# Block 0 of a convolution-and-feed-forward kernel: loads in order of need, weight rounding in three steps, and another product split over the column groups

## Chip, cores, metric

One core of a Trainium2 chip. The metric is the device time of one execution in microseconds, as the median of several. All timed runs are of the state "fast" (granted clock 0.999 to 1.0); single executions are so marked.

## The reference

```
# x (8, 4096, 192), weight (8, 7), w_in (192, 2048), w_out (2048, 192)
w = softmax(weight)                         # over the 7 taps of each of 8 heads
y[b, t, d] = sum_k w[head(d), k] * x[b, t - 6 + k, d]      # causal convolution
h = y @ w_in                                # 32768 tokens
out = (h * clip(h + 3, 0, 6) / 6) @ w_out
```

The weights of the feed-forward part come as float64 and are rounded to float32 on the chip.

## The kernel before

The tokens are worked on in 32 blocks of 1024. In each block VectorE makes the convolution `y`, TensorE makes 16 chunks of `h` (two row groups at a time), ScalarE and VectorE the activation ("Relu", then "gate"), and TensorE the out phase (four column groups of 32 at a time; from block 1 on by seven Strassen products of half-size matrices in place of eight plain ones). Block 0 differs: the weights are still arriving and are rounded in 16 units of 128 x 384 elements: 8 of `w_in`, 8 of `w_out`.

```python
class Rounding:                                  # before: two steps
    def first(self):
        ...
        nc.vector.tensor_scalar(out=self.scale[:], in0=high, ...)     # split: two
        nc.vector.tensor_scalar(out=self.top[:], in0=high, ...)       # instructions
        nc.scalar.activation(over[:], self.scale[:], ACT.Relu, ...)   # three passes
        nc.scalar.activation(self.scale[:], over[:], ACT.Relu, ...)
        nc.scalar.mul(self.rest[:], low, 2.0**-52)
    def second(self):
        nc.vector.scalar_tensor_tensor(out=self.scale[:], ...)        # join: two
        nc.vector.scalar_tensor_tensor(out=self.sig[:], ...)          # instructions
        nc.gpsimd.tensor_tensor(out=self.dst, in0=self.sig[:], in1=self.scale[:].bitcast(F32), op=ALU.mult)
        self.then()                              # w_in units: swap

def swap():      # the halves of a w_in unit change places: two DMAs within SBUF
    nc.sync.dma_start(out=w_in[D2:P, other], in_=w_in[0:D2, own])
    nc.sync.dma_start(out=w_in[0:D2, other], in_=w_in[D2:P, own])

def advance(n):                                  # split and passes of a later unit,
    for _ in range(n):                           # then the join of this one
        begin()
        next(ended).second()
...
    for s in range(K3):                          # first round: four chunks, four banks
        for c, h in early:
            h_mm(0, c, h, s)
    for n, (c, h) in enumerate(early):
        h_out(c, h)                              # Relu and gate
        if n:
            advance(1)
    for p in range(2, NP):                       # the other twelve chunks
        h_unit(0, p)
        advance(1)
        h_unit(0, NP + p)
        if p < 5:
            advance(1)
```

Of the kernel before, what the change touches and what calls it, by code (L numbers as in the profile page):

```python
# [7 lines left out]
ALU = mybir.AluOpType  # L8
# [7 lines left out]
def kernel(  # L16
# [49 lines left out]
    ps = ctx.enter_context(tc.tile_pool(name="ps", bufs=4, space=bass.MemoryType.PSUM))  # L66
    start_pools = ExitStack()
    stg = start_pools.enter_context(tc.tile_pool(name="stg", bufs=2 * NP))
    cnv = start_pools.enter_context(tc.tile_pool(name="cnv", bufs=3))

    def load_x(i):
        b, t0 = i // BPB, (i % BPB) * TB
        x = xs.tile([P, K3, PAD + N], F32, name="x")
        src = xT[b].rearrange("(p s) t -> p s t", s=K3)
        head = PAD if t0 == 0 else 0
        if head:
            nc.vector.memset(x[0:D2, :, 0:PAD], 0.0)
        nc.sync.dma_start(out=x[0:D2, :, head:], in_=src[..., t0 - PAD + head : t0 + N])
        nc.sync.dma_start(out=x[D2:P, :, :], in_=src[..., t0 + N - PAD : t0 + TB])
        return x  # L80


# [4 lines left out]
            in_=weight.unsqueeze(1).to_broadcast([H, GJ, KC]),  # L87
        )

    x_tiles = {0: load_x(0)}  # L90



# [15 lines left out]
    def load_w_in(dma, j):  # L109
        st = stage()  # L110
        for half in range(2):
            dma.dma_start(  # L112
                out=st[half * D2 : (half + 1) * D2].rearrange("p (s f) w -> p s (f w)", s=K3),
                in_=w_in_bits[j + half * NP].rearrange("p s f w -> p s (f w)"),
            )
        return st

    def load_w_out(dma, j):
        st = stage()
        dma.dma_start(  # L120
            out=st[:].rearrange("p (k d) w -> p k (d w)", k=2), in_=w_out_bits[:, j]
        )
        return st
# [6 lines left out]
    class Rounding:  # L130
# [7 lines left out]
        def __init__(self, st, dst, then):  # L138
            self.st, self.dst, self.then = st, dst, then

        def first(self):
            low, high = self.st[:, :, 0], self.st[:, :, 1]
            self.rest = cnv.tile([P, WS], F32, name="rest")
            self.top = cnv.tile([P, WS], U32, name="top")
            self.sig = cnv.tile([P, WS], F32, name="sig")
            self.scale = cnv.tile([P, WS], U32, name="scale")
            over = cnv.tile([P, WS], F32, name="over")
            nc.vector.tensor_scalar(  # L148
                out=self.scale[:], in0=high, scalar1=0x7FF00000, scalar2=None,
                op0=ALU.bitwise_and,  # L150
            )
            nc.vector.tensor_scalar(
                out=self.top[:], in0=high, scalar1=0xFFFFF, scalar2=0x100000,
                op0=ALU.bitwise_and, op1=ALU.bitwise_or,
            )


            nc.scalar.activation(  # L158
                over[:], self.scale[:], ACT.Relu, bias=bias_e[:, 0:1], scale=-1.0
            )  # L160
            nc.scalar.activation(  # L161
                self.scale[:], over[:], ACT.Relu, bias=bias_e[:, 1:2], scale=-8.0
            )
            nc.scalar.mul(self.rest[:], low, 2.0**-52)  # L164

        def second(self):
            nc.vector.scalar_tensor_tensor(
                out=self.scale[:], in0=self.st[:, :, 1], scalar=0x80000000,
                in1=self.scale[:], op0=ALU.bitwise_and, op1=ALU.bitwise_or,
            )  # L170
            nc.vector.scalar_tensor_tensor(
                out=self.sig[:], in0=self.top[:], scalar=2.0**-20, in1=self.rest[:],
                op0=ALU.mult, op1=ALU.add,
            )
            nc.gpsimd.tensor_tensor(
                out=self.dst, in0=self.sig[:], in1=self.scale[:].bitcast(F32), op=ALU.mult
            )
            self.then()
# [17 lines left out]
                out=w_out[:, :, o], in0=w_out[:, :, x], in1=w_out[:, :, y], op=ALU.subtract  # L196
            )

    w_in_st = [load_w_in(nc.scalar if j < 2 else nc.sync, j) for j in range(NP)]
    w_out_st = [load_w_out(nc.sync, j) for j in range(NP)]  # L200

    mx = cst.tile([P, 1], F32, name="mx")
    nc.vector.tensor_reduce(out=mx[:], in_=w_sb[:], axis=AX.X, op=ALU.max)
# [3 lines left out]
    )  # L207
    nc.scalar.activation(e_sb[:], e_sb[:], ACT.Exp)
    sm = cst.tile([P, 1], F32, name="sm")
    nc.vector.tensor_reduce(out=sm[:], in_=e_sb[:], axis=AX.X, op=ALU.add)  # L210
    nc.vector.tensor_scalar_add(sm[:], sm[:], 1e-9)
    nc.vector.reciprocal(sm[:], sm[:])
    c_sb = cst.tile([P, KC], F32, name="c_sb")
    half = cst.tile([P, 1], F32, name="half")
    nc.vector.memset(half[:], 0.5)
# [40 lines left out]
                start=(s == 0), stop=(s == K3 - 1),  # L256
            )

    def h_out(c, h):

        r6 = rs.tile([P, G, N], F32, name="r6")
        nc.scalar.activation(r6[:], h[:], ACT.Relu, bias=half[:], scale=1.0 / 6.0)  # L262
        nc.vector.scalar_tensor_tensor(  # L263
            out=g[:, c % NP, c // NP], in0=r6[:], scalar=1.0, in1=h[:],
            op0=ALU.min, op1=ALU.mult,
        )

    def h_unit(i, c):
        h = banks()
        for s in range(K3):  # L270
            h_mm(i, c, h, s)
        h_out(c, h)

    def dff_half(k):
        return g[:, :, k // G, k % G]
# [13 lines left out]
    def side_by_side(*streams):  # L289
        for mms in zip(*streams):  # L290
            for m in mms:
                m()
# [36 lines left out]
    def out_strassen(i, conv):  # L329

        prod = {
            1: (A11, B11), 2: (A12, B21), 3: (S4, B22), 4: (A22, T4),
            5: (S1, T1), 6: (S2, T2), 7: (S3, T3),
        }

        def product(bank, j, n, q, ks=every):
            return mm(bank, j, *prod[n], q, ks, True, True)

        def three(n, n4, q4):
            bank = banks()[:, 0]  # L340
            side_by_side(
                *[product(bank, q, n, q) for q in range(NQ)], product(bank, NQ, n4, q4)
            )
            return bank

        def piece(dst, q, src, j):
            nc.scalar.copy(  # L347
                out=dst[q * QS : (q + 1) * QS], in_=src[j * QS : (j + 1) * QS]
            )

        def add(out, x, y, op=ALU.add):
            nc.vector.tensor_tensor(out=out, in0=x, in1=y, op=op)  # L352

        def store(c, k, half_):

            xt = ot.tile([P, N], F32, name="xt")
            nc.vector.transpose(out=xt[0:DH], in_=c)  # L357
            for q in range(NQ):
                store_rows(i, k, half_ * NQ + q, xt, q)

        m = slice(0, DH)
        p1, p2, p4, p5, u2, u3 = (cs.tile([DH, N], F32, name=f"c{k}") for k in range(6))
        b = three(1, 2, 0)
        nc.scalar.copy(out=p1[:], in_=b[m])  # L364
        piece(p2, 0, b, NQ)
        s_sums(every, (2, 4), 4)
        b = three(4, 2, 1)
        nc.scalar.copy(out=p4[:], in_=b[m])  # L368
        piece(p2, 1, b, NQ)
        for u in conv[:4]:  # L370
            u()
        n = NP // 4
        b = banks()[:, 0]
        side_by_side(*[product(b, j, 2, 2, range(j * n, (j + 1) * n)) for j in range(4)])
        last = p2[2 * QS : 3 * QS]
        piece(p2, 2, b, 0)
        for j in range(1, 4):
            add(last, last, b[j * QS : (j + 1) * QS])
        add(p2[:], p1[:], p2[:])
        store(p2[:], 0, 0)  # L380
        for u in conv[4:]:
            u()
        b7 = three(7, 5, 0)
        piece(p5, 0, b7, NQ)
        b = three(6, 5, 1)
        piece(p5, 1, b, NQ)
        add(u2[:], p1[:], b[m])
        add(u3[:], u2[:], b7[m])
        add(p4[:], u3[:], p4[:], ALU.subtract)
        store(p4[:], 1, 0)  # L390
        b = three(3, 5, 2)
        piece(p5, 2, b, NQ)
        add(u2[:], u2[:], b[m])
        add(u2[:], u2[:], p5[:])
        store(u2[:], 0, 1)
        add(u3[:], u3[:], p5[:])
        store(u3[:], 1, 1)

    def s_sums(pairs, which, width):

# [11 lines left out]
    for j in range(4):  # L412
        units += [w_out_unit(j, w_out_st[j]), w_in_unit(4 + j, w_in_st[4 + j])]
    units += [w_out_unit(j, w_out_st[j]) for j in range(4, NP)]
    begun = iter(units)
    ended = iter(units)

    def begin():
        u = next(begun, None)
        if u:  # L420
            u.first()

    def advance(n):
        for _ in range(n):
            begin()
            next(ended).second()

    with tc.manual_schedule():
        begin()
        begin()  # L430
        nc.vector.tensor_tensor(
            out=c_sb[:], in0=e_sb[:], in1=sm[:].to_broadcast([P, KC]), op=ALU.mult
        )
        next(ended).second()
        next(ended).second()
        conv0 = conv_units(0, [slice(s, s + 1) for s in range(K3)])
        for s in range(K3):
            for u in conv0[s * KC : (s + 1) * KC]:
                u()
            advance(1) if s else begin()  # L440
        x_tiles[1] = load_x(1)


        early = [(c, banks()) for p in range(2) for c in (p, NP + p)]
        for s in range(K3):
            for c, h in early:
                h_mm(0, c, h, s)
        for n, (c, h) in enumerate(early):
            h_out(c, h)
            if n:  # L450
                advance(1)
        for p in range(2, NP):
            h_unit(0, p)
            advance(1)
            h_unit(0, NP + p)
            if p < 5:
                advance(1)
        y_tiles.pop(0)
        w_out_sums()
        start_pools.close()  # L460
# [52 lines left out]
```

## Time and profile before

| | before |
|---|---|
| time, median | 2548.4 us |
| TensorE waits for the first swap, then starts its long run | 32.12 us |
| out phase of block 0 starts | 92.20 us |
| block 0 ends | 133.60 us |
| 31 blocks of | 77.59 us |
| last matmul to the end | 8.3 us |

The table is read from the chain of waits (the work that ended last, followed back from the last instruction, at each step to what released it) and from the busy times by stage; the prediction shows the lines. From 133.60 us to the last matmul TensorE never waits, so a change that takes no matmuls away can win only ahead of that and behind it.

### The profile page before, as it was taken

Reading aid. Unit: us, or ns where it says so; the run is one execution under the profiler, and the core shown is the slowest. Engines: PE = TensorE matmul, PEld = TensorE weight load, DVE = VectorE, ACT = ScalarE, POOL = GpSimd, SP = SyncE. Lnnn points to the kernel's source line nnn. Section 1 sums busy time; section 2 is a strip of 40 time slices with the busy share of each in tenths; the row PEclk is TensorE's granted clock in tenths of the full one; section 3 lists DMA queues with packets and bytes.
Section 4 is the critical chain, followed back from the end, with each engine's and each line's share of the span. In section 5 each row is a group of like instructions: output and inputs, shape, how many; then the busy total and the mean of one; then the engine's idle time right before and its main releaser. Section 6 shows DMA issues by size and latency. Waiting matters only on the chain.

```text
span 2547.2 us, 37923 instructions
## 1 busy us (share of the span) xinstructions
PE 2495.4 (98%) x16944; PEld 945.9 (37%) x16944; DVE 1923.2 (76%) x1640; ACT 740.9 (29%) x810; POOL 28.6 (1%) x24
## 2 busy tenths in 40 slices
PE   4899999999999999999999999999999999999998
PEld 2233333333333333333333333333333333333333
DVE  5667777777778777877777787777787787777775
ACT  3333222332222332223332223322233322233222
POOL 1300000000000000000000000000000000000000
PEclk9999999999999999999999999999999999999999
DMA  6001110011110111101111101111001111011100
GB/s 142 16 17 26 26 26 7 19 26 26 26 22 8 23 26 26 26 8 21 24 26 26 26 5 22 26 26 26 12 18 23 26 26 26 7 20 26 26 13 13
DMA packets 223155, 60.91 MB, mean 24 GB/s; under 512 B 204560, under 2 KB 210704, under 8 KB 222992
## 3 DMA queue, kind: packets, MB, share of 16 engines
q1 hardware_dynamic: 222088, 57.70, 12.1%
q8 instruction: 133, 2.18, 0.4%
q10 hardware_dynamic: 904, 0.79, 0.2%
q14 instruction: 30, 0.25, 0.0%
HBM read 31.72 MB, written 25.17 MB: 22 GB/s over the span
## 4 chain that ended last, share of the span: by engine, by line
PE 97%; ACT 1%; DMA 1%; issue 1%; DVE 0%; ACTq 0%; SPq 0%; DVEq 0%
PE banks L254 51%; PE banks L281 46%; ACT r L262 0%; DMA stage<-in_moe_w_in_dram 0%; DMA w_in<-w_in 0%; DMA stage<-in_moe_w_out_dram 0%; ACT over L158 0%; ACT rest L164 0%; ACT scale L161 0%; DVE g L263 0%; DVE scale L148 0%; SPq L112 0%; DVE c L352 0%; ACTq L112 0%; ACTq L85 0%
## 5 line engine op out<-in xcount | busy, mean ns | idle before, releaser
L254 PE MATMUL banks<-y,w_in 64*128 64x512 f32 x6144 | 1334.4, 591 | 43.4 <-DVE y L231 23.7
L263 DVE SCALAR_TENSOR_TENSOR g<-r,banks 128x1024 f32<-128x1024 f32 x512 | 623.3, 1218 | 428.6 <-ACT r L262 428.6
L254 PEld LDWEIGHTS banks<-y,w_in 64*128 64x128 f32 x6144 | 598.1, 187 | 779.2 <-issue 751.7
L262 ACT ACTIVATE r<-banks,half 128x1024 f32<-128x1024 f32 x512 | 569.9, 1114 | 789.5 <-PE banks L254 723.8
L281 PE MATMUL banks<-g,w_out 128*32 128x512 f32 x6336 | 739.4, 593 | 0.0
L281 PE MATMUL banks<-s,w_out 128*32 128x512 f32 x4464 | 643.6, 592 | 0.0
L281 PEld LDWEIGHTS banks<-g,w_out 128*32 128x32 f32 x6336 | 215.4, 110 | 516.1 <-issue 491.5
L231 DVE SCALAR_TENSOR_TENSOR y<-x,c_sb,y 128x1536 f32<-128x1536 f32 (+1 forms) x204 | 356.1, 1745 | 6.1
L281 PEld LDWEIGHTS banks<-s,w_out 128*32 128x32 f32 x4464 | 183.5, 110 | 296.8 <-issue 296.5
L347 ACT COPY c<-banks 32x512 f32<-32x512 f32 x186 | 107.7, 579 | 601.6 <-PE banks L281 600.9
L352 DVE TENSOR_TENSOR c<-c,banks 32x512 f32<-32x512 f32 (+1 forms) x186 | 127.4, 685 | 138.9 <-ACT c L347 133.8
L409 DVE TENSOR_TENSOR g<-g 128x1024 f32<-128x1024 f32 x124 | 151.9, 1225 | 4.3
L409 DVE TENSOR_TENSOR s<-g 128x1024 f32<-128x1024 f32 x124 | 151.9, 1225 | 4.2
L409 DVE TENSOR_TENSOR s<-g,s 128x2048 f32<-128x2048 f32 x62 | 139.1, 2284 | 0.0
L409 DVE TENSOR_TENSOR s<-s,g 128x2048 f32<-128x2048 f32 x62 | 139.0, 2284 | 0.0
L357 DVE STREAM_TRANSPOSE xt<-c 96x512 f32<-96x512 f32 x124 | 87.7, 707 | 4.3
L352 DVE TENSOR_TENSOR c<-c,c 96x512 f32<-96x512 f32 x124 | 83.9, 677 | 3.2
L364 ACT COPY c<-banks 96x512 f32<-96x512 f32 x31 | 18.0, 582 | 184.0 <-PE banks L281 184.0
L368 ACT COPY c<-banks 96x512 f32<-96x512 f32 x31 | 18.0, 582 | 176.4 <-PE banks L281 176.4
L227 DVE TENSOR_SCALAR y<-x,c_sb 128x1536 f32<-128x1536 f32 (+1 forms) x34 | 57.4, 1689 | 0.0
L158 ACT ACTIVATE over<-scale,bias_e 128x384 f32<-128x384 uint32 x16 | 9.9, 617 | 41.0 <-DVE scale L148 41.0
L325 DVE STREAM_TRANSPOSE xt<-banks 128x512 f32<-128x512 f32 x3 | 2.1, 715 | 17.1 <-PE banks L281 17.1
(25 smaller groups left out, 80.3 us busy)
## 6 DMA issues: line engine op xcount, KB each, us to landing
out_dram<-xt SPq DMA_DIRECT2D x384, 64.0 KB, 2.0
x<-in_x_dram SPq DMA_DIRECT2D x56, 388.5 KB, 5.6
x<-in_x_dram SPq DMA_DIRECT2D x8, 384.0 KB, 4.5
stage<-in_moe_w_out_dram SPq DMA_DIRECT2D x8, 384.0 KB, 7.6
stage<-in_moe_w_in_dram SPq DMA_DIRECT2D x12, 192.0 KB, 6.1
w_in<-w_in SPq DMA_DIRECT2D x16, 96.0 KB, 2.2
stage<-in_moe_w_in_dram ACTq DMA_DIRECT2D x4, 192.0 KB, 8.7
w_sb<-in_weight_dram ACTq DMA_DIRECT2D x1, 1.8 KB
```

The costliest lines, as they stand in the source:

```text
L227: nc.vector.tensor_scalar(out=y[:, part], in0=x[:, part, 0:N], scalar1=c, scalar2=None, op0=ALU.mult)
L231: nc.vector.scalar_tensor_tensor(out=y[:, part], in0=x[:, part, k : k + N], scalar=c, in1=y[:, part], op0=ALU.mult, op1=ALU.add,)
L254: nc.tensor.matmul(out=h[:, k], lhsT=w_in[r, slot, s, :], rhs=y[r, s, :], start=(s == 0), stop=(s == K3 - 1),)
L262: nc.scalar.activation(r6[:], h[:], ACT.Relu, bias=half[:], scale=1.0 / 6.0)
L263: nc.vector.scalar_tensor_tensor(out=g[:, c % NP, c // NP], in0=r6[:], scalar=1.0, in1=h[:], op0=ALU.min, op1=ALU.mult,)
L281: lambda p=p: nc.tensor.matmul(out=bank[j * QS : (j + 1) * QS], lhsT=w_out[:, p, w, cols], rhs=x[:, p], start=(first and p == ps_[0]), sto ...
L347: nc.scalar.copy(out=dst[q * QS : (q + 1) * QS], in_=src[j * QS : (j + 1) * QS])
L352: nc.vector.tensor_tensor(out=out, in0=x, in1=y, op=op)
L357: nc.vector.transpose(out=xt[0:DH], in_=c)
L364: nc.scalar.copy(out=p1[:], in_=b[m])
L368: nc.scalar.copy(out=p4[:], in_=b[m])
L409: nc.vector.tensor_tensor(out=o[:, r], in0=x[:, r], in1=y[:, r], op=op)
```

## The change

Three parts. The loads: weight units in the order in which they are rounded, x of block 0 in three pieces of each half, the first beside unit 0. The rounding: three steps (split, clamp, join) that work on three different units in one turn. The out phase: another product has its last third spread over the four column groups, so that less work follows the last matmul. Its core:

```diff
-    x_tiles = {0: load_x(0)}
+    load_x0(nc.scalar, 0)                       # one third of x of block 0
...
-    w_in_st = [load_w_in(nc.scalar if j < 2 else nc.sync, j) for j in range(NP)]
-    w_out_st = [load_w_out(nc.sync, j) for j in range(NP)]
+    for j in range(NP):
+        w_in_st[j] = load_w_in(nc.sync, j)
+        if j == 1:
+            for s in range(1, K3):
+                load_x0(nc.sync, s)
+        if j >= 4:
+            w_out_st[j - 4] = load_w_out(nc.sync, j - 4)
+    for j in range(4, NP):
+        w_out_st[j] = load_w_out(nc.sync, j)
...
+            r6 = h_relu(h)
+            if slot >= 2 and n < len(units):
+                clamp(n + 1)                    # ScalarE: three passes
+                units[n].join()                 # VectorE: two, then POOL's multiply
+                split(n + 2)                    # VectorE: two
+                n += 1
+            h_gate(c, h, r6)
...
-        side_by_side(*[product(b, j, 2, 2, range(j * n, (j + 1) * n)) for j in range(4)])
+        side_by_side(*[product(b, j, 5, 2, range(j * n, (j + 1) * n)) for j in range(4)])
...
-        b = three(3, 5, 2)
-        piece(p5, 2, b, NQ)
+        b = three(3, 2, 2)
         add(u2[:], u2[:], b[m])
-        add(u2[:], u2[:], p5[:])
-        store(u2[:], 0, 1)
-        add(u3[:], u3[:], p5[:])
-        store(u3[:], 1, 1)
+        store(u2, 0, 1)
+        add(p2[last], p1[last], b[NQ * QS :])
+        store(p2, 0, 0, range(2, NQ))
```

More of the change, by code (lines that the diff above doesn't have):

```diff
@@ L68, with x_source, load_x @@
     stg = start_pools.enter_context(tc.tile_pool(name="stg", bufs=2 * NP))
-    cnv = start_pools.enter_context(tc.tile_pool(name="cnv", bufs=3))
-    def load_x(i):
+    cnv = start_pools.enter_context(tc.tile_pool(name="cnv", bufs=4))
+    def x_source(i):
         b, t0 = i // BPB, (i % BPB) * TB
-        x = xs.tile([P, K3, PAD + N], F32, name="x")
         src = xT[b].rearrange("(p s) t -> p s t", s=K3)
         head = PAD if t0 == 0 else 0
+        return head, src[..., t0 - PAD + head : t0 + N], src[..., t0 + N - PAD : t0 + TB]
+    def load_x(i):
+        x = xs.tile([P, K3, PAD + N], F32, name="x")
+        head, lower, upper = x_source(i)
         if head:
             nc.vector.memset(x[0:D2, :, 0:PAD], 0.0)
-        nc.sync.dma_start(out=x[0:D2, :, head:], in_=src[..., t0 - PAD + head : t0 + N])
-        nc.sync.dma_start(out=x[D2:P, :, :], in_=src[..., t0 + N - PAD : t0 + TB])
+        nc.sync.dma_start(out=x[0:D2, :, head:], in_=lower)
+        nc.sync.dma_start(out=x[D2:P, :, :], in_=upper)
         return x
@@ L88, with load_x0 @@
         )
-    x_tiles = {0: load_x(0)}
+    x_tiles = {0: xs.tile([P, K3, PAD + N], F32, name="x")}
+    nc.vector.memset(x_tiles[0][0:D2, :, 0:PAD], 0.0)
+    def load_x0(dma, s):
+        head, lower, upper = x_source(0)
+        dma.dma_start(out=x_tiles[0][0:D2, s, head:], in_=lower[:, s])
+        dma.dma_start(out=x_tiles[0][D2:P, s, :], in_=upper[:, s])
+    load_x0(nc.scalar, 0)
     w_in = cst.tile([P, NC, K3, P], F32, name="w_in")
@@ L139, in __init__, with split @@
             self.st, self.dst, self.then = st, dst, then
-        def first(self):
-            low, high = self.st[:, :, 0], self.st[:, :, 1]
-            self.rest = cnv.tile([P, WS], F32, name="rest")
+        def split(self):
+            high = self.st[:, :, 1]
             self.top = cnv.tile([P, WS], U32, name="top")
+            self.scale = cnv.tile([P, WS], U32, name="scale")
             self.sig = cnv.tile([P, WS], F32, name="sig")
-            self.scale = cnv.tile([P, WS], U32, name="scale")
-            over = cnv.tile([P, WS], F32, name="over")
             nc.vector.tensor_scalar(
@@ L155, in first, with clamp, join @@
             )
+        def clamp(self):
             nc.scalar.activation(
-                over[:], self.scale[:], ACT.Relu, bias=bias_e[:, 0:1], scale=-1.0
+                self.sig[:], self.scale[:], ACT.Relu, bias=bias_e[:, 0:1], scale=-1.0
             )
             nc.scalar.activation(
-                self.scale[:], over[:], ACT.Relu, bias=bias_e[:, 1:2], scale=-8.0
+                self.scale[:], self.sig[:], ACT.Relu, bias=bias_e[:, 1:2], scale=-8.0
             )
-            nc.scalar.mul(self.rest[:], low, 2.0**-52)
-        def second(self):
+            nc.scalar.mul(self.sig[:], self.st[:, :, 0], 2.0**-52)
+        def join(self):
             nc.vector.scalar_tensor_tensor(
@@ L171, in second @@
             nc.vector.scalar_tensor_tensor(
-                out=self.sig[:], in0=self.top[:], scalar=2.0**-20, in1=self.rest[:],
+                out=self.sig[:], in0=self.top[:], scalar=2.0**-20, in1=self.sig[:],
                 op0=ALU.mult, op1=ALU.add,
@@ L197, in w_out_sums @@
             )
-    w_in_st = [load_w_in(nc.scalar if j < 2 else nc.sync, j) for j in range(NP)]
-    w_out_st = [load_w_out(nc.sync, j) for j in range(NP)]
+    w_in_st, w_out_st = {}, {}
+    for j in range(NP):
[7 more added lines that the diff above has]
+        w_out_st[j] = load_w_out(nc.sync, j)
     mx = cst.tile([P, 1], F32, name="mx")
@@ L209 @@
     sm = cst.tile([P, 1], F32, name="sm")
-    nc.vector.tensor_reduce(out=sm[:], in_=e_sb[:], axis=AX.X, op=ALU.add)
-    nc.vector.tensor_scalar_add(sm[:], sm[:], 1e-9)
-    nc.vector.reciprocal(sm[:], sm[:])
     c_sb = cst.tile([P, KC], F32, name="c_sb")
@@ L257, in h_mm, with h_relu, h_gate @@
             )
-    def h_out(c, h):
+    def h_relu(h):
         r6 = rs.tile([P, G, N], F32, name="r6")
         nc.scalar.activation(r6[:], h[:], ACT.Relu, bias=half[:], scale=1.0 / 6.0)
+        return r6
+    def h_gate(c, h, r6):
         nc.vector.scalar_tensor_tensor(
@@ L271, in h_unit @@
             h_mm(i, c, h, s)
-        h_out(c, h)
+        h_gate(c, h, h_relu(h))
     def dff_half(k):
@@ L352, in add, with store @@
             nc.vector.tensor_tensor(out=out, in0=x, in1=y, op=op)
-        def store(c, k, half_):
+        def store(c, k, half_, qs=range(NQ)):
             xt = ot.tile([P, N], F32, name="xt")
-            nc.vector.transpose(out=xt[0:DH], in_=c)
-            for q in range(NQ):
+            r = slice(qs[0] * QS, (qs[-1] + 1) * QS)
+            nc.vector.transpose(out=xt[r], in_=c[r])
+            for q in qs:
                 store_rows(i, k, half_ * NQ + q, xt, q)
@@ L373, in out_strassen @@
         b = banks()[:, 0]
-        side_by_side(*[product(b, j, 2, 2, range(j * n, (j + 1) * n)) for j in range(4)])
-        last = p2[2 * QS : 3 * QS]
-        piece(p2, 2, b, 0)
+        side_by_side(*[product(b, j, 5, 2, range(j * n, (j + 1) * n)) for j in range(4)])
+        last = slice(2 * QS, 3 * QS)
+        piece(p5, 2, b, 0)
         for j in range(1, 4):
-            add(last, last, b[j * QS : (j + 1) * QS])
-        add(p2[:], p1[:], p2[:])
-        store(p2[:], 0, 0)
+            add(p5[last], p5[last], b[j * QS : (j + 1) * QS])
+        first = slice(0, 2 * QS)
+        add(p2[first], p1[first], p2[first])
+        store(p2, 0, 0, range(2))
         for u in conv[4:]:
@@ L388, in out_strassen @@
         add(u3[:], u2[:], b7[m])
+        add(u2[:], u2[:], p5[:])
         add(p4[:], u3[:], p4[:], ALU.subtract)
-        store(p4[:], 1, 0)
-        b = three(3, 5, 2)
-        piece(p5, 2, b, NQ)
+        store(p4, 1, 0)
+        add(u3[:], u3[:], p5[:])
+        store(u3, 1, 1)
+        b = three(3, 2, 2)
         add(u2[:], u2[:], b[m])
-        add(u2[:], u2[:], p5[:])
-        store(u2[:], 0, 1)
-        add(u3[:], u3[:], p5[:])
-        store(u3[:], 1, 1)
+        store(u2, 0, 1)
+        add(p2[last], p1[last], b[NQ * QS :])
+        store(p2, 0, 0, range(2, NQ))
     def s_sums(pairs, which, width):
@@ L414, with split, clamp @@
     units += [w_out_unit(j, w_out_st[j]) for j in range(4, NP)]
-    begun = iter(units)
-    ended = iter(units)
-    def begin():
-        u = next(begun, None)
-        if u:
-            u.first()
-    def advance(n):
-        for _ in range(n):
-            begin()
-            next(ended).second()
-    with tc.manual_schedule():
-        begin()
-        begin()
+    def split(n):
+        if n < len(units):
+            units[n].split()
+    def clamp(n):
+        if n < len(units):
+            units[n].clamp()
+    with tc.manual_schedule():
+        split(0)
+        clamp(0)
+        nc.vector.tensor_reduce(out=sm[:], in_=e_sb[:], axis=AX.X, op=ALU.add)
+        nc.vector.tensor_scalar_add(sm[:], sm[:], 1e-9)
+        nc.vector.reciprocal(sm[:], sm[:])
         nc.vector.tensor_tensor(
@@ L433 @@
         )
-        next(ended).second()
-        next(ended).second()
         conv0 = conv_units(0, [slice(s, s + 1) for s in range(K3)])
-        for s in range(K3):
-            for u in conv0[s * KC : (s + 1) * KC]:
-                u()
-            advance(1) if s else begin()
+        for k, u in enumerate(conv0):
+            if k == 3:
+                units[0].join()
+                split(1)
+                clamp(1)
+            elif k and k % KC == 0:
+                n = k // KC
+                units[n].join()
+                split(n + 1)
+                clamp(n + 1)
+            u()
+        units[3].join()
+        split(4)
+        clamp(4)
+        split(5)
         x_tiles[1] = load_x(1)
@@ L447 @@
                 h_mm(0, c, h, s)
-        for n, (c, h) in enumerate(early):
-            h_out(c, h)
-            if n:
-                advance(1)
-        for p in range(2, NP):
-            h_unit(0, p)
-            advance(1)
-            h_unit(0, NP + p)
-            if p < 5:
-                advance(1)
+        n = 4
+        for slot in range(2 * NP):
+            c = slot // 2 + slot % 2 * NP
+            if slot < len(early):
+                h = early[slot][1]
+            else:
+                h = banks()
+                for s in range(K3):
+                    h_mm(0, c, h, s)
+            r6 = h_relu(h)
+            if slot >= 2 and n < len(units):
+                clamp(n + 1)
+                units[n].join()
+                split(n + 2)
+                n += 1
+            h_gate(c, h, r6)
+        assert n == len(units)
         y_tiles.pop(0)
```

## The prediction

> **What bounds the kernel now.** I read the chain of waits first. Here are its pieces in order of time (start, length, what):
>
> ```profile
> 32.12 10.39 PE banks L254 x35
> ...
> 92.27 41.34 PE banks L281 x384
> 133.60 41.40 PE banks L254 x192
> 175.01 36.19 PE banks L281 x336
> ...
> 2502.65 36.23 PE banks L281 x336
> 2538.91 0.59 ACT c L347
> ```
>
> From 133.60 to 2538.91 us TensorE never waits: 31 blocks of 41.40 + 36.19 = 77.59 us, 2405.3 us in all. What a change can win without taking matmuls away lies in the other 143 us: block 0, which ends at 133.60 though its matmuls need only 41.4 + 41.3 = 82.7 us, and the 8.3 us after the last matmul (span 2547.2). Next, the busy time by stage (length; then PE, PEld, DVE, ACT and POOL with their counts):
>
> ```profile
> 0.00:32.12 32.12, 2.04 (x3) 0.50 (x3) 18.66 (x40) 8.17 (x14) 3.78 (x7) 1.00 0.99 232
> 32.12:45.06 12.94, 12.94 (x48) 9.99 (x48) 6.94 (x12) 3.79 (x5) 1.00 (x1) 1.00 0.38 92
> 45.06:92.20 47.14, 33.79 (x146) 13.98 (x145) 30.55 (x56) 29.13 (x44) 10.14 (x11) 1.00 0.08 18
> ```
>
> There are three losses. (1) 32.1 us in which TensorE has next to nothing and DMA is busy 0.99 of the time. (2) A first round of four chunks that takes 12.9 us. (3) 47.1 us for the other twelve chunks, which at 41.40 / 16 = 2.59 us each need 31.0; so 16.1 us are lost there. What ends (1) is seen in the timeline and in the answer for the swap's line:
>
> ```profile
> 23.98 0.53 SPq L184 DMA_DIRECT2D w_in<-w_in  x1
> 32.12 21.24 PE L254 MATMUL banks<-y,w_in 64*128 64x512 f32 x82 [6.43 <-DMA w_in<-w_in]
> DMA to landing us min/median/max: 2.1/2.1/8.1
> ```
>
> The first chunk needs the half-swapped copy of weight unit 0. That swap is issued at 23.98, after all 20 weight loads on the same queue, and lands after 8.1 us instead of the usual 2.1, because it stands behind the loads under way. Loss (3) is this loop, once for each chunk, in the chain of waits from 49 to 60 us:
>
> ```profile
> 50.28 0.36 DVE scale L148
> ...
> 50.67 0.63 ACT over L158
> ...
> 51.38 0.62 ACT scale L161
> 52.00 0.45 ACT rest L164
> 52.45 1.01 ACT r L262
> ...
> 53.54 1.07 issue
> 54.62 0.36 DVE scale L148
> ```
>
> 54.62 - 50.28 = 4.34 us a turn. VectorE splits a unit, ScalarE makes three passes over it, only then the chunk's own Relu, then VectorE's gate, then the next split. No engine is full (DVE 30.6, ACT 29.1 of 47.1 us): it is a loop of latency.
>
> **What the Trainium skill says.** "DMA: Bandwidth & Descriptors", section "Queues, rings and completion order", says that each DMA engine consumes its ring in order: the trace agrees (swap 8.1 us behind loads, 2.1 us alone). "SBUF — State Buffer", section "Door 1: The DMA port swizzle", says a transfer over 64 partitions gets the bandwidth of one over 32: while x and w_in (64 partitions) load I see 207 to 224 GB/s, while w_out (128 partitions) loads up to 374. So the order of the loads leaves their sum alone. The same page, "Who interferes with whom", says that a VectorE instruction with two SBUF inputs, or in a 2-port mode, and a GpSimd instruction exclude each other, the later one waiting. The trace agrees:
>
> ```profile
> 15.96 0.55 DVE L167 SCALAR_TENSOR_TENSOR scale<-stage,scale 128x384 uint32<-128x384 uint32 x1
> 16.12 1.24 POOL L175 TENSOR_TENSOR w_in<-sig,scale 128x384 f32<-128x384 f32 x1 [15.68 <-DVE sig L171]
> 16.43 1.35 DVE L171 SCALAR_TENSOR_TENSOR sig<-top,rest 128x384 f32<-128x384 uint32 x1
> ...
> 96.83 1.22 DVE L263 SCALAR_TENSOR_TENSOR g<-r,banks 128x1024 f32<-128x1024 f32 x1
> 96.99 1.01 POOL L175 TENSOR_TENSOR w_out<-sig,scale 128x384 f32<-128x384 f32 x1 [3.91 <-DVE sig L171]
> ```
>
> POOL took 1.24 instead of 1.01 us behind L167, and L171, normally 0.55, took 1.35 behind POOL. The gate, which reads PSUM, passed beside POOL untouched.
>
> **The change, part by part.**
>
> *Loads.* x of block 0 comes in six pieces in place of two, its first third beside unit 0. VectorE starts about 3 us earlier (estimate: 655 KB at 0.215 MB/us from 3.4 us, about 1.2 us to land, so 7.7 instead of 10.65) and the convolution of block 0 ends near 32 in place of 36.37 us. But the matmuls of the last third began only near 40, so they did not wait for it. The swap stays behind all loads, whose bytes are the same: it lands near 32 again. Gain: 0, give or take 0.7 us. The first round, slow at its start (0.43 us a matmul until 36.9, 0.215 after), stays at 12.9 us and ends near 45.
>
> *Rounding.* A turn now holds on ScalarE the Relu first and then the three passes of the next unit; on VectorE the join of one unit, the split of the one after next, the gate. Each waits only for work of the turn before, so the longest engine counts, not the loop. Start to start in the old trace: ScalarE 1.02 + 0.71 + 0.52 + 0.45 = 2.70 us; VectorE 0.47 + 0.47 + 0.27 + 0.27 + 1.14 to 1.22 = 2.62 to 2.70; TensorE 2.59. TensorE starts the fifth chunk near 45.0 and can stay four banks ahead, so at 2.7 us the gates do not hold it: it reaches the out phase at 45.1 + 12 x 2.59 = 76.1 to 76.5 instead of 92.2. **Gain 15.9 us.**
>
> The catch is the lock. The old order had the gate after the join, so POOL's multiply met nothing. In the new one the multiply of the unit just joined meets the two split instructions: 384 elements in 0.35 us with starts 0.27 us apart is over one element a cycle of "VectorE: DVE Perf Modes", section "Mode 2×_2P", so these hold both ports. From the two old collisions POOL asks for the lock 0.07 to 0.15 us after its start, which is 0.63 us after the start of the join's last instruction: at 0.70 to 0.78. The second split begins at 0.74. If POOL gets in between, that split waits some 1.0 us less the overlap: the turn is 0.94 + 0.27 + about 1.05 + 0.15 + 1.14 = 3.55 us. Then the gate that frees the bank of the first out matmul ends at 45.7 + 11 x 3.55 = 84.8, out phase at 85: **gain 7.2 us.**
>
> *Product split.* Both versions issue 336 matmuls a block (five rounds of 64 and one of 16): nothing gained or lost per block. VectorE gets two more instructions (11 adds and 5 transposes for 10 and 4), 1.4 us on 59.9 of 77.6; ScalarE one copy less. The adds moved ahead fit: in the last but one block VectorE idled 3.90 us before the last round's copy, and the new ones take 2 x 0.7. At the very end, before: copy, two adds, transpose, add, transpose, six stores issued 0.5 us apart, the last issued at 2544.23. After: add, transpose (ready near 2540.4), add, transpose (2541.7), three stores then one, the last issued near 2541.85. **Gain 2.4 us.**
>
> Sum: 15.9 + 2.4 = 18.3 (2530.1 us) without the lock, 7.2 + 2.4 = 9.6 (2538.8 us) with it.
>
> **Rivals.** (a) TensorE is the new bound of the rounding stage, 2530. For: the sums of 2.59 to 2.70. Against: the collision. (b) VectorE with the lock, 2539. For: POOL won the port between two back-to-back VectorE instructions at 16.43. Against: there it asked 0.2 us before the next one started, here they tie. (c) ScalarE: the third pass now writes the tile that the second reads; if it waits for its end, the turn is 2.9 us, the out phase starts near 77.6, 2531.5. (d) An earlier start: were the swap to land with the first loads, up to 10 us more, 2520; nothing in the diff moves the swap. (e) A new wait in every block (a bank freed late by the longer tail of adds): 1 us would cost 31. Against: banks have 5 us or more to spare.
>
> **Range and chances.** (a) with (c) and (b) I hold almost equal, (b) slightly ahead; so 2535, with 2528 and 2541.5 outside the two cases by a couple of us for the swap. 2% is 51 us: block 0 and the tail together lose only 143 - 83 = 60 us, of which 32 are loading, so faster by 2% has 1 in 100; slower by 2% needs a wait of 1.6 us in each block, as rare.
>
> **What would show it.** In the changed profile: the out phase of block 0 starts near 76 (a) or 85 (b); the second split instruction takes 0.35 us or about 1.3; TensorE's long run starts near 32, released by the swap; blocks stay at 77.59; the span ends about 5.9 us after the last matmul. I am wrong if the first long matmul run starts before 30 or after 34, if blocks change by over 0.1 us, or if turns take 4 us or more.

## The result, and the profile after

The changed kernel takes 2536.57 us (median of 6, 2535.78 to 2536.74) beside 2548.45 for the kernel before: 11.9 us less, ratio 0.9952, 95% interval 0.9939 to 0.9965. Here and below a ratio is the mean time of one kernel's fast runs over that of the other's of the same rounds, so not quite the ratio of the medians. That is inside the predicted range, and same by the 2% measure. All outputs are right.

The chain of waits of the changed kernel, in order of time:

```profile
23.69 7.43 DMA w_in<-w_in
31.16 17.84 PE banks L272 x70
...
52.59 1.08 DVE top L163
...
56.01 1.07 DVE top L163
...
59.41 1.07 DVE top L163
...
81.59 41.34 PE banks L302 x384
122.93 41.40 PE banks L272 x192
164.33 36.19 PE banks L302 x336
...
2491.97 36.23 PE banks L302 x336
2528.23 0.70 DVE c L373
```

Blocks are unchanged (41.40 + 36.19). Block 0 ends at 122.93 us, 10.67 earlier. The swap still ends the wait for TensorE's long run. What is new is `DVE top L163`, the second split instruction, which stands in the chain once in each turn (the work for one chunk and one unit), every 3.41 us, with 1.07 us. The busy times by stage (length; PE, PEld, DVE, ACT, POOL; PEclk, which is the granted clock of TensorE, DMA share, GB/s), up to the long run, the first round, the other twelve chunks, and the end behind the last matmul:

```profile
0.00:31.16 31.16, 2.04 (x2) 0.50 (x2) 23.89 (x47) 8.61 (x14) 3.33 (x7) 1.00 0.99 240
31.16:43.57 12.41, 12.41 (x47) 9.71 (x47) 3.50 (x7) 3.96 (x6) 1.04 (x1) 1.00 0.42 96
43.57:81.52 37.95, 33.41 (x146) 14.13 (x145) 37.95 (x56) 32.86 (x46) 11.50 (x11) 1.00 0.09 21
...
2528.23:2534.10 5.87, 0.00 (x0) 0.00 (x0) 2.79 (x4) 0.00 (x0) 0.00 (x0) 0.95 0.48 72
```

The three stages give 0.96 us (32.12 to 31.16), 0.53 (12.94 to 12.41) and 9.19 (47.14 to 37.95); the end gives 2.43 (8.30 to 5.87). That is 13.1 us between the two profiled executions, of which the one before lay at the long end of its kernel's times and the one after at the short end; the medians differ by 11.9. The 0.53 us of the first round are the pace of its first matmuls: their pairs start 0.86 us apart at first and 0.43 us later, and the slow stretch lasted about 3.8 us here (31.16 to about 34.9) in place of 4.8 (32.12 to 36.9). No part of the change aims at that.

In the twelve-chunk stage VectorE is now busy 37.95 of 37.95 us, and yet the sum of its work is not that long. One turn in the timeline of the changed kernel (start, length, engine) shows why:

```profile
58.13 0.54 DVE L180 SCALAR_TENSOR_TENSOR scale<-stage,scale 128x384 uint32<-128x384 uint32 x1
...
58.60 0.55 DVE L184 SCALAR_TENSOR_TENSOR sig<-top,sig 128x384 f32<-128x384 uint32 x1
59.07 0.35 DVE L159 TENSOR_SCALAR scale<-stage 128x384 uint32<-128x384 uint32 x1
59.22 1.05 POOL L188 TENSOR_TENSOR w_out<-sig,scale 128x384 f32<-128x384 f32 x1 [2.36 <-DVE sig L184]
59.34 1.15 DVE L163 TENSOR_SCALAR top<-stage 128x384 uint32<-128x384 uint32 x1
...
60.41 1.21 DVE L284 SCALAR_TENSOR_TENSOR g<-r,banks 128x1024 f32<-128x1024 f32 x1
```

Join (L180, L184), first split (L159, 0.35 us), then POOL's multiply starts, and the second split, which does as much as the first, takes 1.15 us: it ends 0.22 us after POOL does (60.49 and 60.27). A busy engine is not always a working one: 0.8 us of each turn's "busy" time is a wait that the profile books as work. Over all 16 units, the answers for this line before and after:

```profile
L152 DVE TENSOR_SCALAR top<-stage x16: 351/355/355, 10.9 to 90.7; 128x384 uint32<-128x384 uint32 x16
```

```profile
L163 DVE TENSOR_SCALAR top<-stage x16: 348/1153/1169, 7.3 to 76.4; 128x384 uint32<-128x384 uint32 x16
```

(ns, shortest, median and longest of 16; the line number changed with the text.) These durations are what the theory has to explain.

### The profile page after: what moved, and what is told of

The parts are those of the page before. It is cut to its first block, busy times and chain, and to the rows that moved or that the text cites. A ratio compares the mean times of both kernels' runs of the same rounds, so it can differ in the third digit from the quotient of the medians.

```text
span 2534.1 us, 38016 instructions
## 1 busy us (share of the span) xinstructions
PE 2494.5 (98%) x16944; PEld 945.7 (37%) x16944; DVE 1973.7 (78%) x1702; ACT 724.8 (29%) x779; POOL 25.5 (1%) x24
## 4 chain that ended last, share of the span: by engine, by line
PE 97%; DMA 1%; DVE 1%; issue 0%; SPq 0%; ACTq 0%; ACT 0%; DVEq 0%
PE banks L272 51%; PE banks L302 46%; DVE top L163 0%; DMA stage<-in_moe_w_out_dram 0%; DMA w_in<-w_in 0%; DMA stage<-in_moe_w_in_dram 0%; DMA x<-in_x_dram 0%; DVE g L284 0%; DVE scale L180 0%; DVE sig L184 0%; SPq L125 0%; DVE scale L159 0%; DVE c L373 0%; ACTq L89 0%; ACT r L279 0%
## 5 line engine op out<-in xcount | busy, mean ns | idle before, releaser
L272 PE MATMUL banks<-y,w_in 64*128 64x512 f32 x6144 | 1333.5, 591 | 33.7 <-DVE y L249 15.8
L302 PE MATMUL banks<-g,w_out 128*32 128x512 f32 x6336 | 909.8, 593 | 0.0
L302 PE MATMUL banks<-s,w_out 128*32 128x512 f32 x4464 | 697.3, 592 | 0.0
L302 PEld LDWEIGHTS banks<-g,w_out 128*32 128x32 f32 x6336 | 253.9, 110 | 479.0 <-issue 454.4
L302 PEld LDWEIGHTS banks<-s,w_out 128*32 128x32 f32 x4464 | 196.3, 110 | 333.9 <-issue 333.9
L368 ACT COPY c<-banks 32x512 f32<-32x512 f32 x155 | 89.6, 578 | 406.8 <-PE banks L302 406.1
L373 DVE TENSOR_TENSOR c<-c,banks 32x512 f32<-32x512 f32 (+1 forms) x217 | 148.9, 686 | 63.2 <-PE banks L302 44.5
L379 DVE STREAM_TRANSPOSE xt<-c 96x512 f32<-96x512 f32 (+2 forms) x155 | 109.4, 706 | 5.3
L373 DVE TENSOR_TENSOR c<-c,c 64x512 f32<-64x512 f32 (+1 forms) x124 | 81.2, 675 | 1.5
L163 DVE TENSOR_SCALAR top<-stage 128x384 uint32<-128x384 uint32 x16 | 16.9, 1054 | 0.0
```

Of the source, the lines that this page charges most:

```text
L272: nc.tensor.matmul(out=h[:, k], lhsT=w_in[r, slot, s, :], rhs=y[r, s, :], start=(s == 0), stop=(s == K3 - 1),)
L302: lambda p=p: nc.tensor.matmul(out=bank[j * QS : (j + 1) * QS], lhsT=w_out[:, p, w, cols], rhs=x[:, p], start=(first and p == ps_[0]), sto ...
L368: nc.scalar.copy(out=dst[q * QS : (q + 1) * QS], in_=src[j * QS : (j + 1) * QS])
L373: nc.vector.tensor_tensor(out=out, in0=x, in1=y, op=op)
L379: nc.vector.transpose(out=xt[r], in_=c[r])
```

## The experiments

The theory: of the change's parts the rounding brings some 9 us and the out phase 2.4; the rounding would bring 7 more if POOL's multiply did not take the port between the two splits; and what holds the start is the swap behind the loads. Three kernels have one part of the change each. The others alter the changed kernel.

### out_alone

The kernel before with the out phase of the diff.

> The kernel before with only the out phase of the changed kernel. My theory: nothing in the blocks, which stay at 77.59 us; only the end is shorter, 2.4 us (span from the last matmul to the end 5.9 instead of 8.3), so 2546.0 us. Rival: the two more VectorE instructions a block cost something in each of 31 blocks; then blocks of over 77.6 us and a time at or above 2548.4.

Measured: 2546.13 us (5 runs, 2545.54 to 2546.85) beside 2548.64: 2.5 us less (ratio 0.9990, interval 0.9978 to 1.0003, so not clear of zero by the times alone). The profile is clear: the stretch from the last matmul to the end is 5.97 us (2539.03 to 2545.00) in place of 8.30, and the blocks stay at 77.59. The rival falls.

### loads_alone

The kernel before with the diff's loads.

> The kernel before with only the new order of the loads and x in six pieces. Theory of the prediction: no gain, because the swap of unit 0 still stands behind all loads: the long run of TensorE starts within 0.7 us of 32.1 and the time is 2548.4 +- 0.7. In the changed kernel that run started at 31.16, 1.0 us earlier. Rival: the order itself brings that 1 us, then 2547.4, and the end of the VectorE convolution of block 0, 4 us earlier or more, brings nothing further. Second rival: VectorE's head start is handed on to the rounding: 2545 or less.

Measured: 2547.83 us (5 runs) beside 2548.64: 0.8 us less, interval 0.9984 to 1.0010. The long run starts at 31.27 in place of 32.12 us and is again released by the swap. The convolution of block 0 ends at 30.99 in place of 36.37 us, and the twelve-chunk turns stay at 4.33 (gate ends 48.63, 52.96, 57.30): VectorE's head start is not handed on. The start moved as the first rival had it, but that the order of the loads moved it is not shown: with the old loads the long run starts between 31.53 us (rounding_alone) and 32.48 (rounding_again_2), with the new ones between 31.16 (the changed kernel) and 32.88 (multiply_on_vector), and the interval of the times includes no change at all. During the loading the mean rate was 239 GB/s up to the start here and 232 before; why is not shown.

### rounding_alone, and three repeats

The kernel before with the three-step rounding.

> The kernel before with only the three-step rounding (old loads, old out phase). Theory: turns of 3.41 us as in the changed kernel, of which about 0.8 is the second split instruction waiting for POOL (1.15 instead of 0.35 us); the out phase of block 0 starts near 82.6 (1 us later than the 81.6 of the changed kernel, for the later start), so 2548.4 - 9.6 = 2538.8. Rival: without the loads in order of need the units arrive too late and turns are longer, out phase at 85 or later, 2541 or more.

Measured: 2538.56 us (5 runs) beside 2548.64. The profiled execution (2539.56 us) has turns of 3.41 us, second splits of 1.157 us in the median, and the out phase at 82.78. So the rounding alone brings 9 to 10 us, and late loads do not lengthen its turns. But two of the five executions took 2532.03 and 2533.95, and no profile of those was kept. Three repeats were to catch one:

> The rounding alone once more, one execution, because two of its five executions took 2532.0 and 2534.0 us and three 2538.6 to 2539.7. If the race for the port between POOL's multiply and the second split is decided in two ways, an execution of about 2532 shows second splits of 0.35 us in most turns, and one of about 2539 shows 1.15 us in all. Rival: the short executions come from an earlier start of TensorE's long run (by 5 us or more), with turns of 3.41 as ever.

> As rounding_again_1, a second execution: near 2532 with short second splits, or near 2539 with long ones.

> As rounding_again_1, a third execution: near 2532 with short second splits, or near 2539 with long ones.

Measured: 2539.35, 2539.28 and 2539.00 us (one execution each); in all three, all but the first and sixth of the 16 second splits took 1.15 us or more. No short execution was caught. That the two short ones won the race for the port fits their times but is not shown; it stays open.

### gate_first

```diff
                 units[n].join()
-                split(n + 2)
-                n += 1
             h_gate(c, h, r6)
+            if slot >= 2 and n < len(units):
+                split(n + 2)
+                n += 1
```

> The changed kernel with one exchange in each turn: join, gate, split in place of join, split, gate, so that POOL's multiply runs beside the gate, which reads PSUM. Lock theory: both split instructions take 0.35 us, turns fall from 3.41 to 2.6 to 2.75, TensorE becomes the bound, the out phase of block 0 starts near 74.7 in place of 81.6: 2536.6 - 6.9 = 2529.7. Rival, ScalarE bounds the turn (its third pass waits for its second): turns of 2.9, out phase near 76.4, 2531.4. Rival, latency of the chain and not the lock: the split now comes later, the passes on it too; turns stay at 3.4 or more, 2536.6 or more.

Measured: 2529.58 us (4 runs, 2529.13 to 2529.94) beside 2548.26, ratio 0.9927 (0.9910 to 0.9943): 7.0 us less than the changed kernel, and the out phase starts at 74.85. Its timeline, with the gate where the splits were:

```profile
55.55 0.56 DVE L184 SCALAR_TENSOR_TENSOR sig<-top,sig 128x384 f32<-128x384 uint32 x1
...
56.02 1.23 DVE L284 SCALAR_TENSOR_TENSOR g<-r,banks 128x1024 f32<-128x1024 f32 x1
56.19 1.00 POOL L188 TENSOR_TENSOR w_out<-sig,scale 128x384 f32<-128x384 f32 x1 [1.60 <-DVE sig L184]
...
57.15 0.37 DVE L159 TENSOR_SCALAR scale<-stage 128x384 uint32<-128x384 uint32 x1
57.42 0.37 DVE L163 TENSOR_SCALAR top<-stage 128x384 uint32<-128x384 uint32 x1
```

POOL and the gate run beside each other at their own length; both splits are short. (Four of the 16 second splits, ahead of this loop, still take 1.15 us; the exchange does not touch them.) The stage of twelve chunks:

```profile
43.87:74.85 30.98, 30.98 (x144) 15.78 (x144) 30.51 (x56) 30.27 (x45) 11.14 (x12) 1.00 0.11 26
```

TensorE is busy in all of it: 30.98 / 12 = 2.58 us a chunk. Both rivals fall. The same instructions in another order are worth 7 us.

### multiply_on_vector

```diff
-            nc.gpsimd.tensor_tensor(
+            nc.vector.tensor_tensor(
                 out=self.dst, in0=self.sig[:], in1=self.scale[:].bitcast(F32), op=ALU.mult
             )
```

> The changed kernel with the multiply of the rounding moved from POOL to VectorE, after the join: more work for the engine that fills the turn (0.47 to 0.55 us each), but nothing on POOL to wait for. Lock theory: the second split falls from 1.15 to 0.35 us, the turn is 3.41 - 0.80 + 0.55 = 3.15 to 3.2, the out phase starts near 79.5, 2 us earlier: 2534.5. Rival, no lock (the second split is slow for another reason, its two operations or its operands): the turn grows by 0.5 to 3.9, the out phase starts near 86.5, 2541.5.

```profile
60.00 0.55 DVE L180 SCALAR_TENSOR_TENSOR scale<-stage,scale 128x384 uint32<-128x384 uint32 x1
60.47 0.55 DVE L184 SCALAR_TENSOR_TENSOR sig<-top,sig 128x384 f32<-128x384 uint32 x1
61.05 0.56 DVE L188 TENSOR_TENSOR w_out<-sig,scale 128x384 f32<-128x384 f32 x1
61.53 0.35 DVE L159 TENSOR_SCALAR scale<-stage 128x384 uint32<-128x384 uint32 x1
61.80 0.35 DVE L163 TENSOR_SCALAR top<-stage 128x384 uint32<-128x384 uint32 x1
62.07 1.21 DVE L284 SCALAR_TENSOR_TENSOR g<-r,banks 128x1024 f32<-128x1024 f32 x1
63.20 0.55 DVE L180 SCALAR_TENSOR_TENSOR scale<-stage,scale 128x384 uint32<-128x384 uint32 x1
```

The turn is 63.20 - 60.00 = 3.20 us, as the lock theory had it: the engine that fills the turn got more to do and the turn grew shorter. The second split has no length of its own to explain. The time did not follow: 2536.22 us (4 runs), 0.4 less than the changed kernel and not 2. In this profile TensorE's long run started at 32.88 us, 1.7 later than in the changed kernel, and its slow pace lasted until about 38.7 us in place of 34.9, so that the first Relu came at 43.77 in place of 41.05. From there to the out phase (82.11 and 81.52) it is 38.34 us in place of 40.47: the 2 us expected are there, and what is missing was lost ahead of them. Why the start was late I did not settle.

### tiny_copy_on_pool

```diff
+            nc.gpsimd.tensor_copy(out=tiny[:], in_=self.sig[:, 0:1])
             nc.gpsimd.tensor_tensor(
```

> The changed kernel with one more instruction on POOL ahead of each multiply: a copy of one column of what the join wrote, which nothing uses. It makes POOL longer and asks for the multiply's port about 0.1 us or more later. Lock theory with a race: the second split has begun by then, keeps the port, and POOL waits for it instead; second splits of 0.35 to 0.5 us, turns of 2.65 to 2.85, out phase of block 0 near 75, time near 2530. Rival: the port goes to POOL whenever it comes during the two splits, or the small copy itself takes the place of the multiply in the queue: second splits stay at 1.15 us or more, turns 3.4 or more, 2536.6 or more.

Measured: 2530.22 us (4 runs) beside 2548.62, ratio 0.9928 (0.9911 to 0.9944). From its timeline:

```profile
59.13 0.35 DVE L160 TENSOR_SCALAR scale<-stage 128x384 uint32<-128x384 uint32 x1
59.34 0.18 POOL L189 COPY tiny<-sig 128x1 f32<-128x1 f32 x1 [1.31 <-DVE sig L185]
59.40 0.35 DVE L164 TENSOR_SCALAR top<-stage 128x384 uint32<-128x384 uint32 x1
59.48 1.15 POOL L190 TENSOR_TENSOR w_in<-sig,scale 128x384 f32<-128x384 f32 x1
```

Now the second split starts 0.08 us ahead of the multiply, takes 0.35 us, and the multiply takes 1.15 in place of 1.00. In the changed kernel the multiply started 0.12 us ahead. The loser waits, and which one it is turns on 0.2 us. A useless instruction on POOL is worth 6.3 us; this is no way to write a kernel, but it shows that the wait turns on which of the two starts first, with the VectorE program left as it was.

### swaps_among_loads

The last ten weight loads are issued later in the program, six behind the swap of unit 0 and four behind that of unit 1.

```diff
                 units[0].join()
+                load_more()                     # w_out 2, w_in 6, w_out 3, w_in 7
                 split(1)
...
                 units[n].join()
+                if n == 1:
+                    load_rest()                 # w_out 4 to 7
```

> The changed kernel with the last ten weight loads issued later in the program, so that the swap of unit 0 stands before twelve... that is before all of them, and that of unit 1 before the last four. Theory: what starts TensorE's long run is the swap behind the loads; it then lands near 20 instead of 31, and the bound of the first round becomes VectorE's convolution of the last third of x (30.5): the first round ends near 34 in place of 43.6 and the out phase of block 0 starts near 72.6 in place of 81.6: 2536.6 - 9 = 2527.6. Rival: the loads are what binds, later ones now arrive late for their units and the gain is given back: less than 3 us, 2533.6 or more.

Measured: 2531.65 us (4 runs) beside 2548.26, ratio 0.9934: 4.9 less than the changed kernel, not 9. TensorE's lines in its timeline:

```profile
20.95 4.13 PE L272 MATMUL banks<-y,w_in 64*128 64x512 f32 x8 [2.83 <-DMA w_in<-w_in]
27.97 12.51 PE L272 MATMUL banks<-y,w_in 64*128 64x512 f32 x46 [2.89 <-DMA w_in<-w_in]
```

The swap of unit 0 lands near 21, as expected. But the next wait is for the swap of unit 1, until 27.97: its multiply had ended at 17.98, and it was issued at 21.18, behind the six loads. And the matmuls run at half their pace again from 27.97 until 31.7 (starts of a pair 0.86 us apart, then 0.43). So the first round ends near 38.4 and not at 34, and the out phase starts at 76.46. The theory was right that the swap held the start; what took its place was mis-seen.

### gate_first_and_swaps

> Both of the exchanges: gate before split, and swaps among the loads. If the two losses are one after the other, the gains add: first round to 34, then TensorE's own pace of 2.59 us a chunk, out phase of block 0 near 65.8, 2536.6 - 15.8 = 2520.8. Rival: with the earlier start the units or their swaps come too late for their chunks, and the sum is short of that by 3 us or more: 2524 or more.

Measured: 2524.89 us (4 runs) beside 2548.26, ratio 0.9907 (0.9892 to 0.9922): 11.7 less than the changed kernel. The two parts had given 7.0 and 4.9 alone, so they add; both fall on the path one after the other. Short of the 15.8 expected by what swaps_among_loads fell short.

### best

As gate_first_and_swaps, with the swap of unit 1 ahead of seven loads in place of four, and chunks 0 and 8 brought further before unit 1 is needed:

```diff
-                load_more()                     # two pairs
+                load_more()                     # one pair: w_out 2, w_in 6
...
-                    load_rest()                 # w_out 4 to 7
+                    load_rest()                 # w_out 3, w_in 7, w_out 4 to 7
...
-        for s in range(K3):
-            for c, h in early:
-                h_mm(0, c, h, s)
+        for pair in (early[:2], early[2:]):
+            for s in range(K3 - 1):
+                for c, h in pair:
+                    h_mm(0, c, h, s)
+        for c, h in early:
+            h_mm(0, c, h, K3 - 1)
```

> Gate before split, and swaps among the loads, with two mends: the swap of unit 1 now stands before seven loads in place of four, and the first round does two thirds of chunks 0 and 8 before it asks for unit 1. In gate_first_and_swaps the first round was held by the swap of unit 1 (landed at 28.1) and by matmuls at 0.43 us after the pause, and ended at 39.1. Theory: the swap of unit 1 lands near 25, only the last third of the convolution (30.2) is then waited for, the first round ends at 34.5 to 36.5 and all that follows is TensorE's own pace: 2524.9 - 3.5 = 2521.4. Rival: matmuls at half rate take the gain back: 2524 or more.

Measured: 2521.39 us (4 runs, 2521.28 to 2521.71) beside 2548.82, ratio 0.9892 (0.9876 to 0.9909). It beats both kernels: 27.4 us below the kernel before, 15.2 below the changed one. Its stages:

```profile
0.00:20.97 20.97, 2.04 (x2) 0.50 (x3) 13.90 (x32) 6.83 (x11) 2.29 (x6) 1.00 0.93 209
20.97:36.20 15.23, 13.06 (x46) 8.00 (x47) 13.50 (x22) 5.76 (x9) 2.09 (x2) 1.00 0.94 241
36.20:67.31 31.11, 31.11 (x145) 15.91 (x145) 30.64 (x56) 30.41 (x45) 11.13 (x12) 1.00 0.20 46
```

TensorE is busy from 36.20 on, and the first round now runs inside the loading (DMA share 0.94). TensorE's last wait inside the first round is 0.30 us for the convolution, at 30.63; 1.88 us more pass until the first gate frees a bank.

## Why the prediction was right

- **The blocks.** Predicted unchanged at 77.59 us, with 1.4 us more for VectorE: found (61.30 us of VectorE a block in blocks 2 to 4 for 59.87 before, TensorE without a gap).
- **The end.** Predicted 2.4 us; 2.43 in the profile, 2.5 in out_alone.
- **The turn.** Two cases were given almost equal chances, TensorE's pace (out phase near 76) and, slightly ahead, the lock (near 85). It was the lock: the changed kernel shows it, and gate_first, multiply_on_vector and tiny_copy_on_pool take it away in three ways, each with short second splits in that loop. The case without it was right in size: gate_first starts the out phase at 74.85 and takes 2529.6, where the prediction had 2530.1 for that case.
- **The size of the lock.** The turn was put at 3.55 us and is 3.41; the stage gave 9.2 us for 7.2. The mis-sized term is the wait of the second split for POOL: the sum has 1.05 + 0.15 = 1.20 us from its start to that of the gate, and it took 1.07 (59.34 to 60.41), which is nearly all of the 0.14 us a turn. The last two of the turns, which have no split any more, are shorter still (2.07 us), which I left out.
- **The start.** Predicted at 32 give or take 0.7; it came at 31.16, just outside, and the first round, put at 12.9 us, took 12.41. Both are small misses, and both may be scatter: kernels with the same loads start up to 1.7 us apart, and the slow pace of the first matmuls lasts longer in one profile than in another.
- **The mean.** 2535 was a mean of two cases, 2530.1 and 2538.8. That it lies only 1.6 us from the result is luck: in the two profiled executions the stage gave 2.0 us more than the second case had it, the start 1.0 and the first round 0.5, all with the same sign (by the medians 2.3 in all), and this moved the result from the second case towards the mean.

What is not settled: two short executions of rounding_alone, the late start in multiply_on_vector, and whether the new order of the loads brings anything by itself.

## What to carry to other kernels

When two engines share a port, a pipelined order that looks free in sums of durations can lose to one that puts an instruction without that port beside the other engine's work; compare the duration of the same instruction before and after, since the profile books such a wait as busy time. A transfer that the first matmul needs should be issued ahead of loads that are needed later, not behind them, even if it can be issued only when a unit is ready (4.9 us here). Before moving a bound, ask what the second thing in line waits for: here the next swap held back part of what the first one gave.

## What the Trainium skill lacked or had wrong

- "SBUF — State Buffer", section "Who interferes with whom", gives the shared pair to whichever instruction issues first. Recorded starts agree in the cases here, but the page has no word on how close it is: with the multiply recorded 0.12 us ahead of the second split the split took 1.15 us, with 0.08 us behind it took 0.35 and the multiply 1.15. Nor does it say that the recorded length of a split is more than the time for which it holds the port: the multiply started at 59.22 inside the first split's 59.07 to 59.42 and lost at most 0.05 us.
- "TensorE: Matmul & The Clock Gate", section "Part 1: The HAM clock gate", gives a warm-up of about 3.4 us of time that varies by run. Here the half pace lasted from about 3.1 us in loads_alone (31.27 to 34.4) over 4.8 in the kernel before (32.12 to 36.9) to 5.8 in multiply_on_vector (32.88 to 38.7), and in swaps_among_loads a first burst of 4.1 us (20.95 to 25.08) ran at half pace throughout and the next one, 2.9 us later, began so again. The pace is read from the starts of the matmuls; the PEclk column, 1.00 or 0.90 in the stretches shown, does not show it.
